# First block's inversion put ahead of the second block's preparation, its transfers on ScalarE's queue, and the last two steps' output sums taken one by one

## Chip, cores and metric

The kernel runs on one NeuronCore of a Trainium2 chip. The metric is the device time of one execution in microseconds (us). Five engines take part: PE (TensorE), DVE (VectorE), ACT (ScalarE), POOL (GpSimd) and SP (SyncE, which here only issues DMAs). Each engine works through its own list of instructions in the order of the program, and waits at the head of that list when an operand isn't there.

## What is computed

Three stages follow each other: a recurrence over 768 tokens for 4 x 8 heads of size 40, a router with eight experts, and a dense feed-forward layer.

```python
for t in range(S):                                   # recurrence, per head: state is 40 x 40
    y[:, :, t] = einsum('bhd,bhde->bhe', rt, state)
    Sa = einsum('bhde,bhe->bhd', state, at)
    state = state * wt[:, :, None, :] - einsum('bhd,bhe->bhde', Sa, bt) + einsum('bhd,bhe->bhde', vt, kt)
...
x = y.transpose(0, 2, 1, 3).reshape(B * S, H * D)    # 3072 x 320
expert = argmax(x @ w_gate); gate = softmax(x @ w_gate)[expert]
x = gate * (relu(x @ w1[expert]) @ w2[expert])       # at most 768 tokens an expert
h = x @ w_in
out = maximum(0.01 * h, h) @ w_out
```

## The kernel before

**The recurrence** (`attention`) is done in chunks of 32 tokens, so that most of it becomes small matmuls. A *block* i (0 to 5) is a set of four chunks g for both halves hf of the batch, which makes eight *steps* a block, s = 8i + 2g + hf, and 48 in all. A block goes through these stages:

- `load(n, h)` (n = 2i + hf, h the half of the chunks): SP issues the DMAs of w, KB and AE.
- `prep(n, h)`: on DVE two scans over w (L371, L375), a small copy WC (L372), a reciprocal (L373), a product Q (L374); then products on AE (L378, DVE or POOL) and on KB (L381, POOL or DVE).
- `gram(n, g)`: 16 small matmuls (L408), copies into mab (ACT), a DMA mab to Md in HBM, and masks on AE (L423 on DVE, L432 on POOL).
- `inverse_first` (block 0) or `inverse` (the others): Mu is loaded from Md; POOL makes Tt from it (L437); then the triangular inverse of 128 matrices of 32 x 32. For block 0 that is 56 DVE instructions in a row (L445, L447), each needing the one before. The result goes to Td by DMA; of block 0 a part also goes over Ta to Tad.
- `tbl(i, gp)` loads TB from Td. For block 0, `rtl` loads Rt from Tad with four DMAs, and `fix(hf, gp)` (L496, L498, L505) completes TB. Up to here a block's steps can't go on.
- The steps: `rv` (loads), `kbt`, `chain` (L562, copy X, L573 with TB, copies into MV, L590, L594: the state that step s + 2 needs), `output` (L610, L623, masks L631 on DVE or L637 on POOL) and `sums`.

`sums(s)` is called after each odd step and makes the outputs of the steps s and s + 1, that is both halves of the batch, in one run of 32 matmuls into `py` (three banks; half 0 uses banks 0 and 1, half 1 banks 1 and 2). After the last chunk of a block it multiplies py by Wt (L667), and `Router.add` does the routing of those rows: transposes, logits, position in the expert, and for each half two scatters by POOL (L904) into `xs` in HBM. The experts' stage begins by reading `xs` (L1036), when all scatters have landed.

**The order** on each engine comes from a list scheduler (`Sched`). Every `op` has a planned duration, keys that it reads and writes, a due time (`Q.due`, set by `when`), and a time before which it may not be planned (`Q.since`); `Sched.run` places the ops one by one on planned clocks, and `emit` writes them out in that order. So a planned clock decides only the order in which instructions stand on an engine; on the chip each one starts when its engine and its operands allow. In the kernel before, all DMAs of the recurrence are on SP (`QI = 'S'`); `dma` would plan a DMA on ACT at 0.06 us.

The AE and KB tiles have four buffers (n % 4), so blocks i and i + 2 share them; Mu and Tt are single.

Of the kernel before, what the change touches and what calls it, by code (L numbers as in the profile page):

```python
# [26 lines left out]
class Sched:  # L27
# [15 lines left out]
    def op(self, on, dur, fn, r=(), w=(), ring=None, done=0., grp=None, xfer=0., banks=(), sel=False, act=None):  # L43

        i = len(self.ops)
        deps = set()
        for k in r:
            if k in self.w:
                deps.add(self.w[k])
        for k in w:  # L50
            if k in self.w:
                deps.add(self.w[k])
            deps.update(self.r.get(k, ()))
        deps.discard(i)
        for k in r:
            self.r.setdefault(k, set()).add(i)
        for k in w:
            self.w[k] = i
            self.r[k] = set()
        on = on if isinstance(on, dict) else {on: dur}  # L60
        self.ops.append(dict(on=on, fn=fn, deps=deps, ring=ring, done=done, grp=grp, users=0, ps=None, xfer=xfer, banks=list(banks), due=self.due, since=self.since, slack=self.slack, sel=sel, act=act))
        return i
# [172 lines left out]
NV, QI, GS = 1, 'S', 0  # L235
SLACK0, LD0, LDS, PR0, PRS, LATEW, RV0, ZR0, ZRS, GR = 0.244, 0.0, 3.0, 18.956, 0.418, 0, 40.584, 52.618, 7.65, 1
NMV, NRE, NNI, NZ, NWT = 6, 6, 2, 4, 5
VROW = (5, 10)
EI = 'V'


# [34 lines left out]
def attention(ctx, tc, I, R, eng):  # L276
# [4 lines left out]
    Q = Sched(eng)  # L281
    op = Q.op
    V, A, P, T, S = eng
# [6 lines left out]
    def tiles(n, shape, name):  # L290
        return [cp.tile(shape, F32, name=f"{name}{i}") for i in range(n)]

    def copy(E, o, i):
        (E.copy if E is A else E.tensor_copy)(o, i)  # L294
# [4 lines left out]
    def alu(cols, on='VP'):  # L299
        return {e: t for e, t in (('V', .07 + .00104 * cols), ('P', .1 + .00219 * cols)) if e in on}  # L300
# [17 lines left out]
    Mu, Tt = tiles(1, [128, 32, 32], "Mu")[0], tiles(1, [128, 32, 32], "Tt")[0]  # L318
    tmps = tiles(3, [128, 256], "tmp")
    Ta = cp.tile([128, 16, 16], F32, name="Ta")  # L320
    R4 = cp.tile([128, 4, 8, 16], F32, name="Rt")
# [6 lines left out]
    py = ps.tile([128, 3, 512], F32, name="py")  # L328
    Mds = [dr.tile([8, 16, 32, 32], F32, name=f"Md{i}") for i in range(2)]
    Tds = [dr.tile([32, 4, 32, 32], F32, name=f"Td{i}") for i in range(2)]  # L330
    Tad = dr.tile([32, 4, 16, 16], F32, name="Tad")
# [8 lines left out]
        P.memset(maskZ, 0.0)  # L340
        P.iota(maskZ.bitcast(I32)[:, D:D + 1], [[0, 1]], base=NT, channel_multiplier=0)
    def dma(o, i, nb, r, w, on='S'):
        op(on, .48 if on == 'S' else .06, lambda E: E.dma_start(o, i), r, w, xfer=max(.18, nb / 360e3))

    def hold(i, fn):
        pass
# [87 lines left out]
    def inverse_first(i):  # L434

        dma(Mu, Mds[i % 2].rearrange("c u t s -> (c u) t s"), 1 << 19, [('Md', i % 2, c) for c in range(8)], ['Mu'])
        op('P', 1.47, lambda E: (E.affine_select(Tt, Mu, [[-1, 32], [1, 32]], ALU.is_gt, 0.0, base=0, channel_multiplier=0),  # L437
                                 E.memset(Tt.rearrange("u a b -> u (a b)")[:, 0:1024:33], -1.0)), ['Mu'], [('Tt', x) for x in range(3)])
        for x in range(2):
            for k in range(1, 15):  # L440
                m, o, c = 15 - k, 16 * x, 16 * x + k
                tv = tmps[x][:, 0:k * m].rearrange("u (a b) -> u a b", b=m)
                d = alu(k * m, EI)
                tt = Tt[:, o:o + k, c + 1:o + 16]
                op(d, 0, lambda E, tv=tv, k=k, o=o, c=c, m=m: E.tensor_tensor(tv, Mu[:, c:c + 1, c + 1:o + 16].broadcast_to([128, k, m]), Tt[:, o:o + k, c:c + 1].broadcast_to([128, k, m]), ALU.mult),  # L445
                   ['Mu', ('Tt', x)], [('tmp', x)])
                op(d, 0, lambda E, tv=tv, tt=tt: E.tensor_tensor(tt, tt, tv, ALU.subtract), [('tmp', x)], [('Tt', x)])  # L447
        op(ev(256), 0, lambda E: copy(E, Ta, Tt[:, 0:16, 0:16].rearrange("u a b -> u b a")), [('Tt', 0)], ['Ta'])
        dma(Tds[i % 2].rearrange("u q s t -> (u q) s t"), Tt, 1 << 19, [('Tt', x) for x in range(3)], [('Td', i % 2)], QI)
        dma(Tad.rearrange("u q s t -> (u q) s t"), Ta, 1 << 17, ['Ta'], ['Tad'], QI)  # L450

    def when(s):
        Q.due = START + STEP * s
# [1 line left out]
    def inverse(i):  # L455
        dma(Mu, Mds[i % 2].rearrange("c u t s -> (c u) t s"), 1 << 19, [('Md', i % 2, c) for c in range(8)], ['Mu'])
        cuts = [(VROW[0], VROW[1], 'V'), (0, VROW[0], 'V'), (VROW[1], 31, 'P')] if VROW[0] else [(0, VROW[1], 'V'), (0, 0, 'V'), (VROW[1], 31, 'P')]
        tk = [('Tt', x) for x in range(3)]
# [18 lines left out]

    def rtl():
        for q in range(4):
            dma(R4[32 * q:32 * q + 16].rearrange("s m u t -> s (m u) t"), Tad[:, q].rearrange("u s t -> s u t"), 80000, ['Tad'], [('Rt', m, q) for m in range(4)], QI)  # L480

    def tbl(i, gp):
        dma(TB4[:, gp].rearrange("s h u t -> s (h u) t"), Tds[i % 2][16 * gp:16 * gp + 16].rearrange("u q s t -> (q s) u t"), 262144,
            [('Td', i % 2)], [('TB', 2 * gp + h) for h in range(2)], QI if not i else 'S')

    def fix(hf, gp):
        m = 2 * gp + hf
# [148 lines left out]
            if pm:  # L636
                op('P', .62, lambda E, o=o, j=j: E.tensor_tensor(RE[o:o + 64, j], RE[o:o + 64, j], maskP[o:o + 64].unsqueeze(1).broadcast_to([64, 8, 32]), ALU.mult), ['mask'], [('REs', s % NRE, j, par) for par in range(2)])  # L637

    def sums(s):

        i, g, _, _ = info(s)
        def fy(E):
            for p in range(8):
                for j in range(2):
                    for hf in range(2):
                        b, col = place(hf, 2 * p + j)
                        q = 32 * ((g + 2 * hf) % 4)
                        x, z = REs[(s + hf) % NRE], Zs[(s + hf) % NZ]
                        E.matmul(py[q:q + 32, b, col:col + 40], x[:, j, p, :], z[:, p, ZC[j]:ZC[j] + 40], start=True, stop=True)  # L649
        keys = []  # L650
        for u in (s, s + 1):
            keys += [('Zo', u % NZ, h, j) for h in range(2) for j in range(2)] + [('Zs', u % NZ, j) for j in range(2)]
            keys += [('REo', u % NRE, j) for j in range(2)] + [('REs', u % NRE, j, par) for j in range(2) for par in range(2)]
        op('T', 1.45, fy, keys, [('py', hf, g) for hf in range(2)], banks=[('py', b) for b in range(3)], act=4000)
        if g == 3:
            for hf in range(2):
                n = 2 * i + hf
                xk = []
                for bb in range(2):
                    x = (2 * n + bb) % R.NXB  # L660
                    xk.append(x)
                    u = 8 * bb
                    while u < 8 * bb + 8:
                        b, col = place(hf, u)
                        m = min(8 * bb + 8 - u, 12 - col // 40)
                        op('V', .07 + .0416 * m, lambda E, x=x, u=u, b=b, col=col, m=m, bb=bb, n=n:
                           E.tensor_tensor(R.xbs[x][:, 40 * (u - 8 * bb):40 * (u - 8 * bb) + 40 * m], py[:, b, col:col + 40 * m], Wts[n % NWT][:, u:u + m, :].rearrange("p h e -> p (h e)"), ALU.mult),  # L667
                           [('py', hf, k) for k in range(4)] + [('Wt', n % NWT, h, j) for h in range(2) for j in range(2)], [('xb', x, u)], banks=[('py', b)])
                        u += m
                R.add(Q, psum, copy, ev, hf, i, xk)  # L670
# [40 lines left out]
    for m, t in enumerate(NIs):  # L711
        for j in range(2):
            r = RHO[j]
# [4 lines left out]
    for i in range(6):  # L718
        if i < 5:
            for h in range(2):  # L720
                for n in (2 * i + 2, 2 * i + 3):
                    when(8 * i + DPREP[2 * h + n % 2])
                    load(n, h)
                    prep(n, h)
                    for g in (2 * h, 2 * h + 1):
                        gram(n, g)
            inverse(i + 1)
            when(8 * i + DTURN)
            turn(2 * i + 2)
            turn(2 * i + 3)  # L730
        for c in range(8):
            s = 8 * i + c
            _, g, hf, n = info(s)
            when(s)
            if c % 4 == 0:
                tbl(i, g // 2)
                if s == 0:
                    rtl()
            if not i and g % 2 == 0:
                fix(hf, g // 2)  # L740
            Q.since = RV0 if 2 <= s < 8 else 0.
            rv(s)
            Q.since = 0.
            kbt(s)
            chain(s)
            if i == 0 and c < 4:
                Q.since = ZR0 + ZRS * c
                for e in (2 * c, 2 * c + 1):
                    R.zero_region(Q, e, maskZ, [('X', s % 2), ('xbt', 3), ('xbg', 3)] + [('xb', 3, u) for u in range(16)])
                Q.since = 0.  # L750
            when(s + DOUT)
            output(s)
            if s % 2:
                sums(s - 1)
    Q.run()
    Q.emit(lambda: T.matmul(py[:, 2, 320:448], R.one, R.one, start=True, stop=True))
# [704 lines left out]
```

## Time and profile before

| what | value |
|---|---|
| time, median of 3 runs | 1145.58 us (1144.32 to 1146.79) |
| the profiled execution | 1142.32 us, span of its instructions 1140.6 us |
| granted TensorE clock, mean | 0.928 |
| busy, of the span | PE 84%, DVE 69%, ACT 53%, POOL 43% |
| recurrence | from 0 to some 530 us |
| experts and dense layer | from 544 us (read of xs) to the end |

PE's share is high because of the second part, where it hardly pauses. In the recurrence the work of all engines is made of short instructions with waits between them, and there one reads, stretch by stretch, which engine had nothing to do and what ended its wait.

### The profile page before, as it was taken

To read this page: it belongs to the slowest core of one execution; us is meant where nothing else is said; L and a number is where in the kernel's file an instruction comes from. 1 tells how busy PE (TensorE), PEld (TensorE's weight loads), DVE (VectorE), ACT (ScalarE), POOL (GpSimd) and SP (SyncE) were. 2 spreads that over 40 slices of the span, in tenths; PEclk is the share of its full clock that TensorE was granted. 3 is DMA by queue.
4 is the path that set the end of the run, shared out by engine and by line. 5 is a ranking of instruction groups with operands and counts; after the bars stand their busy time and mean duration, and the time that the engine had idled before them with its cause. 6 is when DMAs were issued, how large, how long until landed. Compare 5 with 4: busy or idle time off the path is not lost.

```text
span 1140.6 us, 32337 instructions
## 1 busy us (share of the span) xinstructions
PE 959.8 (84%) x13219; PEld 848.1 (74%) x13219; DVE 791.2 (69%) x1856; ACT 605.2 (53%) x1428; POOL 487.0 (43%) x578
## 2 busy tenths in 40 slices
PE   4565677867777767887789999999999999999997
PEld 3454566656565656675678888989989999999997
DVE  8995878999989968643577777886754444444453
ACT  6135478758768668886434434434433333333343
POOL 7334434646636537121066555561949191010100
PEclk9767789879979889999789999999999999999999
DMA  7539575455445432430666666664211010000000
GB/s 211 195 77 238 137 184 135 134 133 162 133 104 151 131 73 75 107 106 20 205 186 184 200 196 197 198 173 124 81 35 47 24 24 24 1 20 5 24 13 15
DMA packets 134059, 127.82 MB, mean 112 GB/s; under 512 B 90768, under 2 KB 98576, under 8 KB 133904
## 3 DMA queue, kind: packets, MB, share of 16 engines
q1 hardware_dynamic: 131600, 117.79, 36.7%
q0 software_dynamic: 2304, 7.89, 1.9%
q8 instruction: 106, 1.74, 0.6%
q14 instruction: 49, 0.40, 0.1%
HBM read 101.48 MB, written 24.20 MB: 110 GB/s over the span
## 4 chain that ended last, share of the span: by engine, by line
PE 28%; issue 7%; DVE 6%; DMA 4%; POOL 3%; ACT 2%; SPq 1%; DVEq 0%; POOLq 0%; ACTq 0%
PE ph L1015 14%; PE oy L1222 3%; PE oy L1221 3%; PE oy L1220 3%; DMA wc<-cvm 2%; DVE wq L981 1%; PE y L1080 1%; PE y L1083 1%; POOL cvm L1118 1%; POOL cvm L1117 1%; POOL cvm L1119 1%; PE otr L1222 1%; PE otr L1220 1%; PE otr L1221 1%; DMA wa<-cvm 1%
## 5 line engine op out<-in xcount | busy, mean ns | idle before, releaser
L1015 PE MATMUL ph<-xt,wq 128*128 128x512 f32 (+2 forms) x1408 | 311.7, 365 | 4.0 <-DVE xt L1056 3.8
L1015 PEld LDWEIGHTS ph<-xt,wq 128*128 128x128 f32 x1408 | 248.8, 190 | 33.9 <-DVE xt L1056 4.7
L1200 DVE TENSOR_TENSOR gf<-gf,ph 128x512 f32<-128x512 f32 (+1 forms) x112 | 68.3, 610 | 98.9 <-ACT gf L1199 98.5
L1204 DVE TENSOR_TENSOR gl<-gf,gh 128x512 fp32r<-128x512 f32 (+1 forms) x112 | 76.7, 685 | 70.1 <-ACT gh L1203 70.1
L1199 ACT ACTIVATE gf<-ph 128x512 f32<-128x512 f32 (+1 forms) x112 | 60.0, 535 | 109.3 <-PE ph L1015 108.9
L1230 POOL DMA_INDIRECT out_dram<-ob,gid x24 | 23.9, 995 | 218.5 <-ACT ob L1229 213.3
L294 ACT COPY Z<-tr 40x512 f32<-40x512 f32 x192 | 100.4, 539 | 31.1 <-PE tr L610 29.1
L1203 ACT CAST gh<-gf 128x512 fp32r<-128x512 f32 (+1 forms) x112 | 62.7, 559 | 96.6 <-DVE gf L1200 96.6
L1066 ACT ACTIVATE gh<-ph 128x448 fp32r<-128x448 f32 x64 | 34.9, 545 | 121.4 <-PE ph L1015 121.4
L1222 PE MATMUL oy<-wo,gl 128*128 128x320 f32 x288 | 89.2, 310 | 0.2 <-DVE gl L1204 0.2
L1221 PE MATMUL oy<-wo,gh 128*128 128x320 f32 x288 | 88.9, 309 | 0.0
L1220 PE MATMUL oy<-wo,gh 128*128 128x320 f32 x288 | 88.8, 308 | 0.0
L1080 PE MATMUL y<-gh,wo 128*128 128x448 f32 x192 | 73.8, 384 | 6.2 <-DVE Y L1087 6.2
L610 PE MATMUL tr<-ident,MV 128*104 128x128 f32 x384 | 63.8, 297 | 17.8 <-ACT NI L294 6.8
L473 DVE TENSOR_TENSOR Tt<-Tt,tmp 128x30 f32<-128x30 f32 (+22 forms) x275 | 71.8, 290 | 0.7
L432 POOL TENSOR_TENSOR AE<-AE,maskP 32x256 f32<-32x256 f32 x40 | 30.2, 758 | 97.8 <-ACT AE L294 88.3
L1083 PE MATMUL y<-gl,wo 128*128 128x448 f32 x192 | 71.5, 372 | 0.0
L408 PE MATMUL tr<-AE,KB 128*64 128x64 f32 x704 | 37.3, 277 | 35.5 <-DVE AE L378 20.8
L649 PE MATMUL py<-Z,RE 128*32 128x40 f32 x1536 | 47.7, 226 | 22.4 <-DVE RE L631 16.9
L471 DVE TENSOR_TENSOR tmp<-Mu,Tt 128x30 f32<-128x30 f32 (+22 forms) x275 | 64.7, 265 | 0.5
L637 POOL TENSOR_TENSOR RE<-RE,maskP 64x256 f32<-64x256 f32 x24 | 18.6, 776 | 105.7 <-ACT RE L294 103.1
L631 DVE TENSOR_TENSOR RE<-tr,maskP 64x128 f32<-64x128 f32 x144 | 41.4, 288 | 31.7 <-PE tr L623 26.2
(182 smaller groups left out, 2372.1 us busy)
## 6 DMA issues: line engine op xcount, KB each, us to landing
KB<-in_kbT_dram SPq DMA_DIRECT2D x24, 512.0 KB, 6.2
RE<-in_rT_dram SPq DMA_DIRECT2D x48, 256.0 KB, 3.7
AE<-in_aT_dram SPq DMA_DIRECT2D x20, 512.0 KB, 9.2
raw<-in_wo_dram SPq DMA_DIRECT2D x16, 640.0 KB, 4.9
raw<-in_wqa_dram SPq DMA_DIRECT2D x16, 512.0 KB, 5.3
w<-in_wT_dram SPq DMA_DIRECT2D x24, 264.0 KB, 3.0
xs<-xb SPq DMA_DIRECT2D x8, 563.5 KB, 9.9
win<-xs SPq DMA_DIRECT2D x8, 563.5 KB, 8.3
```

What stands on the lines that cost most here:

```text
L294: (E.copy if E is A else E.tensor_copy)(o, i)
L471: op(e, d, lambda E, tv=tv, k=k, lo=lo, h=h, m=m: E.tensor_tensor(tv, Mu[:, k:k + 1, k + 1:].broadcast_to([128, h - lo, m]), Tt[:, lo:h, k ...
L473: op(e, d, lambda E, tv=tv, k=k, lo=lo, h=h: E.tensor_tensor(Tt[:, lo:h, k + 1:], Tt[:, lo:h, k + 1:], tv, ALU.subtract), [('tmp', x)], [t ...
L610: E.transpose(c['t'][0:104, q, :], MV[:, 4 * h + q], ident)
L1015: T.matmul(ph, l, r, start=k == 0, stop=k == 7)
L1080: T.matmul(y[c], hi, gh, start=m == 0, stop=False)
L1083: T.matmul(y[c], hi, gl, start=False, stop=m == 7)
L1200: V.tensor_tensor(gf, gf, ph, ALU.max)
L1204: V.tensor_tensor(gl, gf, gh.bitcast(F32), ALU.subtract)
L1220: T.matmul(o, gh[:, sl], w[:, 0:320], start=m == 0, stop=False)
L1221: T.matmul(o, gh[:, sl], w[:, 320:640], start=False, stop=False)
L1222: T.matmul(o, gl[:, sl], w[:, 0:320], start=False, stop=m == 15)
```

## The change

Three things are changed. `Q.since` is set to `PR1 = 38.6` around the preparation of the second block (i = 1, n = 2 and 3), so that none of its `prep` operations is planned before 38.6 on the planned clock; its loads are not held. The DMAs that follow the first block's inversion (Td, Tad, the first TB, the four Rt) are issued by ACT in place of SP, and a DMA issued by ACT is now planned at 0.48 us as on SP. In `sums` the halves are a parameter: for the steps 46 and 47 it is called after each step's output with one half, 16 matmuls, and its own banks.

```diff
+PR1 = 38.6
...
-        op(on, .48 if on == 'S' else .06, lambda E: E.dma_start(o, i), r, w, xfer=max(.18, nb / 360e3))
+        op(on, .48, lambda E: E.dma_start(o, i), r, w, xfer=max(.18, nb / 360e3))
...
-        dma(Tds[i % 2]..., Tt, 1 << 19, [('Tt', x) for x in range(3)], [('Td', i % 2)], QI)
-        dma(Tad..., Ta, 1 << 17, ['Ta'], ['Tad'], QI)
+        dma(Tds[i % 2]..., Tt, 1 << 19, [('Tt', x) for x in range(3)], [('Td', i % 2)], 'A')
+        dma(Tad..., Ta, 1 << 17, ['Ta'], ['Tad'], 'A')
...  (rtl: QI becomes 'A')
-            [('Td', i % 2)], [('TB', 2 * gp + h) for h in range(2)], QI if not i else 'S')
+            [('Td', i % 2)], [('TB', 2 * gp + h) for h in range(2)], 'A' if not i and not gp else 'S')
...
-    def sums(s):
+    def sums(s, hfs=(0, 1)):
...
-                    for hf in range(2):
+                    for hf in hfs:
...
-        op('T', 1.45, fy, keys, [('py', hf, g) for hf in range(2)], banks=[('py', b) for b in range(3)], act=4000)
+        op('T', 1.45 if len(hfs) > 1 else 1.15, fy, keys, [('py', hf, g) for hf in hfs], banks=[('py', b) for b in (range(3) if len(hfs) > 1 else ((0, 1), (1, 2))[hfs[0]])], act=2000 * len(hfs))
...
                     load(n, h)
+                    Q.since = 0. if i else PR1
                     prep(n, h)
+                    Q.since = 0.
...
-            if s % 2:
+            if s >= 46:
+                sums(46, (hf,))
+            elif s % 2:
                 sums(s - 1)
```

## Rows read from the trace of the kernel before

**Rows 1.** The page: busy tenths of DVE in 40 equal slices of the span.
```profile
DVE  8995878999989968643577777886754444444453
```

**Rows 2.** Windows: stretch, its length, each engine's busy us (instructions); clock, DMA, GB/s.
```profile
39.00:54.50 15.50, 8.19 (x170) 7.97 (x169) 15.03 (x13) 0.61 (x3) 8.10 (x5) 0.92 0.88 318
54.50:65.30 10.80, 3.95 (x55) 3.69 (x55) 10.71 (x59) 3.13 (x9) 3.64 (x3) 0.64 0.05 11
65.30:85.50 20.20, 14.35 (x227) 12.90 (x227) 19.49 (x30) 7.47 (x26) 6.82 (x6) 0.66 0.51 105
85.50:98.10 12.60, 5.18 (x306) 4.59 (x297) 0.00 (x0) 5.43 (x19) 1.40 (x2) 0.67 0.78 197
```

**Rows 3.** Timeline (start us, duration, engine, line; brackets: idle before, releaser): first steps.
```profile
84.86 0.73 PE L496 MATMUL tr<-Rt,TB 16*32 16x16 f32 x64
...
91.97 1.31 PE L573 MATMUL ch<-X,TB 32*32 32x40 f32 x64
...
98.14 0.99 DVE L594 TENSOR_TENSOR MV<-ch,WC 40x320 f32<-40x320 f32 x2 [12.68 <-PE ch L590]
```

**Rows 4.** Timeline of DVE and POOL around the first block's inversion.
```profile
37.79 1.18 DVE L423 TENSOR_TENSOR AE<-ch,maskP 32x128 f32<-32x128 f32 x4
42.35 1.37 POOL L437 TENSOR_SCALAR_AFFINE_SELECT Tt<-Mu 128x1024 f32<-128x1024 f32 x1 [10.65 <-DMA Mu<-Md]
54.51 0.23 DVE L445 TENSOR_TENSOR tmp<-Mu,Tt 128x14 f32<-128x14 f32 x2
58.40 0.69 DVE L378 TENSOR_TENSOR AE<-AE,Q 64x512 f32<-64x512 f32 x1
62.24 2.94 DVE L447 TENSOR_TENSOR Tt<-Tt,tmp 128x14 f32<-128x14 f32 x2
73.41 3.17 DVE L378 TENSOR_TENSOR AE<-AE,Q 64x512 f32<-64x512 f32 x1
73.86 2.17 POOL L381 TENSOR_TENSOR KB<-KB,w 128x1024 f32<-128x1024 f32 x1
```

**Rows 5.** DMA issues between 36 and 100 us: KB each, median us from issue to landing.
```profile
Td<-Tt SPq DMA_DIRECT2D x1, 512.0 KB, 2.7
TB<-Td SPq DMA_DIRECT2D x2, 256.0 KB, 3.5
...
Rt<-Tad SPq DMA_DIRECT2D x4, 32.0 KB, 2.8
```

**Rows 6.** Timeline of SP's queue: DMA issues, from the first block's inversion on.
```profile
65.20 0.33 SPq L343 DMA_DIRECT2D Td<-Tt  x1
...
69.43 4.32 SPq L343 DMA_DIRECT2D Md<-mab  x2
...
74.33 0.47 SPq L343 DMA_DIRECT2D TB<-Td  x1
74.84 3.09 SPq L343 DMA_DIRECT2D Rt<-Tad  x4
...
93.30 1.63 SPq L343 DMA_DIRECT2D Mu<-Md  x1
...
427.15 0.34 SPq L343 DMA_DIRECT2D Mu<-Md  x1
```

**Rows 7.** Timeline of ACT: its first work after the first steps' X copies.
```profile
60.35 0.52 ACT L294 COPY AE<-tr 32x128 f32<-32x128 f32 x2 [20.55 <-PE tr L408]
```

**Rows 8.** Timeline of the recurrence's end: last masks, sums, scatters, read of xs.
```profile
527.38 1.23 DVE L631 TENSOR_TENSOR RE<-tr,maskP 64x128 f32<-64x128 f32 x4 [1.02 <-PE tr L623]
527.50 0.72 POOL L637 TENSOR_TENSOR RE<-RE,maskP 64x256 f32<-64x256 f32 x1 [9.79 <-ACT RE L294]
528.32 1.47 PE L649 MATMUL py<-Z,RE 128*32 128x40 f32 x64
...
536.85 1.08 POOL L904 DMA_INDIRECT xs<-xb,rii  x1 [8.63 <-DVE rm L880]
...
544.36 0.34 SPq L1036 DMA_DIRECT2D win<-xs  x1
```

More of the change, by code (lines that the diff above doesn't have):

```diff
@@ L448, in inverse_first @@
         op(ev(256), 0, lambda E: copy(E, Ta, Tt[:, 0:16, 0:16].rearrange("u a b -> u b a")), [('Tt', 0)], ['Ta'])
-        dma(Tds[i % 2].rearrange("u q s t -> (u q) s t"), Tt, 1 << 19, [('Tt', x) for x in range(3)], [('Td', i % 2)], QI)
-        dma(Tad.rearrange("u q s t -> (u q) s t"), Ta, 1 << 17, ['Ta'], ['Tad'], QI)
+        dma(Tds[i % 2].rearrange("u q s t -> (u q) s t"), Tt, 1 << 19, [('Tt', x) for x in range(3)], [('Td', i % 2)], 'A')
+        dma(Tad.rearrange("u q s t -> (u q) s t"), Ta, 1 << 17, ['Ta'], ['Tad'], 'A')
     def when(s):
@@ L479, in rtl @@
         for q in range(4):
-            dma(R4[32 * q:32 * q + 16].rearrange("s m u t -> s (m u) t"), Tad[:, q].rearrange("u s t -> s u t"), 80000, ['Tad'], [('Rt', m, q) for m in range(4)], QI)
+            dma(R4[32 * q:32 * q + 16].rearrange("s m u t -> s (m u) t"), Tad[:, q].rearrange("u s t -> s u t"), 80000, ['Tad'], [('Rt', m, q) for m in range(4)], 'A')
     def tbl(i, gp):
         dma(TB4[:, gp].rearrange("s h u t -> s (h u) t"), Tds[i % 2][16 * gp:16 * gp + 16].rearrange("u q s t -> (q s) u t"), 262144,
-            [('Td', i % 2)], [('TB', 2 * gp + h) for h in range(2)], QI if not i else 'S')
+            [('Td', i % 2)], [('TB', 2 * gp + h) for h in range(2)], 'A' if not i and not gp else 'S')
     def fix(hf, gp):
@@ L650, in sums @@
         keys = []
-        for u in (s, s + 1):
+        for u in [s + hf for hf in hfs]:
             keys += [('Zo', u % NZ, h, j) for h in range(2) for j in range(2)] + [('Zs', u % NZ, j) for j in range(2)]
             keys += [('REo', u % NRE, j) for j in range(2)] + [('REs', u % NRE, j, par) for j in range(2) for par in range(2)]
-        op('T', 1.45, fy, keys, [('py', hf, g) for hf in range(2)], banks=[('py', b) for b in range(3)], act=4000)
+        op('T', 1.45 if len(hfs) > 1 else 1.15, fy, keys, [('py', hf, g) for hf in hfs], banks=[('py', b) for b in (range(3) if len(hfs) > 1 else ((0, 1), (1, 2))[hfs[0]])], act=2000 * len(hfs))
         if g == 3:
-            for hf in range(2):
+            for hf in hfs:
                 n = 2 * i + hf
```

## The prediction, made before the change was run

> **What bounds the kernel now.** I read the page first, then the windows of the stretch that the change touches, then the timelines of DVE, POOL, SP, PE and ACT in it, and last the end of the recurrence. On the page one looks at DVE: close to full in the first slices and again and again up to the eighteenth, at four to six tenths in the last ten [rows 1]. So the recurrence leans on DVE, the later stages on PE. The change touches only the recurrence; the later stages start when its last scatters have landed, and I let them shift as a whole with it, by one for one.
>
> In the windows one sees what the front looks like. DVE works 15.03 of 15.5 us, 10.71 of 10.8 and 19.49 of 20.2, and then for 12.6 us not at all [rows 2]. The hole from 85.5 to 98.1 is ended by step 0's state update L594, which waited 12.68 us for PE's L590 [rows 3]. Behind that stands this chain: the inversion ran from 54.51 to 65.18, although POOL had finished its Tt at about 43.9 [rows 4]; Td was issued at 65.20 and landed 2.7 us later [rows 5], but the load of TB stood behind other transfers in SP's queue (two Md issues alone took 4.32 us, wait included) and left only at 74.33, the four Rt at 74.84 to 77.93 [rows 6]; PE took up fix at 84.86 and the first steps' L573 at 91.97 [rows 3]. The second block's way is the other limit: its preparation kept DVE busy to 85.5, and its Mu left at 93.30 [rows 2, 6]. From there the blocks follow each other at (427.15 - 93.30)/4 = 83.5 us a block [rows 6]. A block's steps free the buffers for the block after the next, and its inverse must be done before its own steps; so I take a shift of the front to be handed on to the end, whatever the period.
>
> **The edits, one by one.**
>
> *Inversion first.* DVE is free at 37.79 + 1.18 = 38.97; Tt is ready at 42.35 + 1.37 plus a short memset, 43.9 [rows 4]. With the preparation held back DVE waits 5.0 us there for nothing: that is the price. The inversion takes 62.24 + 0.34 - 54.51 less the 0.69 of one product of the preparation that lies in it, 7.4 us (its last pair, 2.94 in the trace, is counted at 0.34, about what the pairs before it took) [rows 4]. So it ends near 51.3 and Td can leave 13.9 us earlier than 65.20. The preparation costs 15.03 + 10.71 + 19.49 = 45.2 us of DVE time in the trace, less 10.0 for the inversion with its held last pair, 35.2; it then ends at 51.3 + 35.2 = 86.5 without the steps, or 89.1 if the 2.6 us that the inversion lost come up elsewhere: 1 to 4 us later than the 85.5 of now.
>
> *Transfers on ACT.* Seven issues move: Td 0.33, Tad, TB 0.47, four Rt 3.09, some 4.3 us at SP's durations [rows 6]. The trace shows no DMA issued by ACT. From below I take nothing, from above those 4.3 us plus a wait of 2.7 us for Td to land at the head of ACT's list. ACT's cover is its idle time of 20.55 us before 60.35 [rows 7]; the chain falls into 51 to 61, so most is hidden. If the cover is gone, what stands behind are the copies of the second block's first grams, and behind these its Md transfers: up to 7 us on the way to Mu. I take zero, as ACT's idle row is the nearest. For the first block I get: Td landed at 51.3 + 0.3 + 2.7 = 54.3, TB at 58.3, Rt, issued one after another from about 55, at 61 [rows 5, 6]. PE's order is the other term: half of the second block's grams may stand ahead of fix, and these come with half of the 35.2 us, at 69. So fix comes at 61 to 69 in place of 84.86, and L573, 7.1 us behind it as now [rows 3], at 68 to 76 in place of 91.97. SP is rid of the same 4.3 us; as its next Md waits for copies and not for SP's time, I give that nothing, and at the most 2 us on Mu.
>
> The Trainium skill ("DMA: Bandwidth & Descriptors", section "Issuing engines are not separate DMA queues") says that transfers of all issuing engines run on the same 16 DMA engines, and that another issuer only saves the time of issuing. By it the move would be worth no more than issue time; the row beside it shows Td landed 6.4 us before TB was issued, which is order in a queue and not bandwidth. The sum below is the same either way.
>
> *What it is worth.* Step 0's chain no longer decides when DVE goes on. The 12.6 us hole is the gain that is there, since steps 0 to 3 then give DVE work during the second block's Mu transfers; the 5.0 us wait at 39 is paid: 12.6 - 5.0 = **7.6 us**. Bounds: more than the hole, if the holding of DVE by POOL goes as well. One product takes 0.69 at 58.40 and 3.17 at 73.41, where POOL's KB product of 2.17 runs beside it [rows 4]; there are four such KB products, so at most 4 x 2.17 = 8.7 us, 16.3 in all. On the other side nothing of the hole is filled and the 5.0 us are paid, with up to 3 us from ACT: 8 us slower. Both unknowns are bounded from both sides; I take the hole alone, since it is read directly.
>
> The Trainium skill ("SBUF — State Buffer", section "SBUF: two separate sides") speaks against the larger value: DVE and POOL share a pair of ports by an exclusive lock, held for a whole instruction. The trace agrees where a product takes 3.17 us beside POOL's 2.17. By that rule the lost time goes with POOL's products wherever they are put, and the gain stays at 7.6.
>
> *Sums taken one by one.* At the end, step 46's mask on POOL ends at 527.50 + 0.72 = 528.22 and step 47's on DVE at 527.38 + 1.23 = 528.61; the 64 matmuls of both take 1.47 [rows 8]. With half 0 alone its 32 are done at 528.22 + 0.74 = 528.96 in place of 529.79: **0.8 us** earlier. The four scatters stand one behind the other on POOL from 536.85 and the last one's landing lets xs be read at 544.36 [rows 8], so the first one's start carries. Bounds: zero, if DVE must wait for bank 1, which PE then fills for half 1; 2 us, if step 46's copies are also put ahead of step 47's. The matmuls stay as many; two more waits cost nothing visible.
>
> *Sum.* 7.6 + 0.8 = 8.4. Against the profiled execution: 1142.3 - 8.4 = 1133.9. That execution is 3.3 us below the median of the runs, so the median comes to **1137** us.
>
> **The rivals.**
>
> *Second block late* (slower). The inversion of block 0 is early, but the second block's Mu is what step 8 waits for. Its preparation ends 1 to 4 us later by itself, and DVE work of steps 0 to 3 comes in between, as do ACT's waits (up to 7). It decides as soon as Mu leaves later than 93.30 by more than the inverse of block 1 gains from having fewer steps beside it. For it: DVE is full before 85.5. Against it: those steps' work is taken out of the time behind Mu. Price: 5.0 of new wait plus 3 on ACT, less 0.8 at the end: about +7, 1153; chance 0.21.
>
> *A wash.* Both limits move by nearly the same, or the new order loses later what it wins at the front: within 3 us, 1143 to 1148; chance 0.15. It includes that the change doesn't do what it says: 38.6 is on the planned clock, and if Mu is planned later than that, the scans still stand ahead of the inversion; then only the 6.4 us of SP's queue remain, on a chain that PE's grams hide.
>
> *Everything recovered.* The hole, and most of the 8.7 us: 16 us, 1129; chance 0.13.
>
> The forecast, 4 to 12 us faster (1133 to 1142), has 0.51.
>
> **How the numbers follow.** 0.2% is 2.3 us, about what a measurement of this kernel can tell from no change. Faster: 0.51 + 0.13 = 0.64. Within: 0.15. Slower: 0.21. The forecast's own range is 1133 to 1142. The range reaches down into the full recovery (1127) and up to where half of the slower case lies (1150), which leaves out some 0.05 below and 0.12 above.
>
> **What would show it.** Right: L445 starts near 44 and Td leaves near 51 to 52 from ACT; fix near 61 to 69; no hole of over 5 us in DVE between 51 and the second block's inverse; Mu of block 1 within some 4 us of 93.3; the last block's Mu about 7 us before 427.15; xs read near 536. Wrong: scans of the preparation ahead of L445; ACT waiting at a DMA while copies of grams stand behind it; block 1's Mu after 100; or an earlier front that the later blocks give back, seen as a Mu of the last block at 427 or later.

## The result, and the profile after

| | before | after |
|---|---|---|
| time, median (lowest to highest), same chip | 1144.95 us (1137.55 to 1149.22, 10 runs) | 1131.84 us (1127.32 to 1137.91, 10 runs) |
| ratio, 95% interval | | 0.9904 [0.9882, 0.9927] |
| the profiled execution, its span | 1142.32, 1140.6 us | 1136.73, 1135.0 us |
| Mu of block 1 / block 2 / block 5 leaves | 93.30 / 185.56 / 427.15 | 90.02 / 177.01 / 419.66 |
| xs read | 544.36 | 539.70 |

By the ratio the changed kernel is faster by 11.0 us of the 1144.95 (8.4 to 13.5 by the interval; the two medians lie 13.1 apart); the forecast was 8.4. The profiled execution of after is 4.9 us above the median of its runs and that of before 2.6 below, so late marks of the two traces compare only to some us. The early ones repeat better: in three kernels with the same order up to the last steps (inv_only, inv_again and no_act, below) Mu of block 1 leaves at 94.15, 93.76 and 93.37. I rest on the early ones. In after all line numbers are one higher up to L638 (L562 is L563), L667 is L668, L904 is L909, L1036 is L1041.

The windows of after in the four stretches of [rows 2] (stretch, length, busy us of PE, PEld, DVE, ACT, POOL; clock, DMA share, GB/s):

```profile
39.00:54.50 15.50, 12.78 (x249) 12.55 (x235) 11.34 (x62) 1.04 (x3) 3.47 (x3) 1.00 0.97 342
54.50:65.30 10.80, 2.72 (x46) 2.59 (x48) 10.52 (x11) 2.49 (x8) 4.05 (x4) 0.52 0.80 153
65.30:85.50 20.20, 13.13 (x303) 11.68 (x300) 17.23 (x31) 8.41 (x28) 8.84 (x7) 0.67 0.63 159
85.50:98.10 12.60, 8.78 (x312) 7.65 (x314) 7.01 (x11) 6.99 (x24) 0.87 (x2) 0.77 0.72 186
```

One sees DVE's hole half filled, 7.01 us where there were none, and the price in the first line, 11.34 us where there were 15.03. Over the four stretches DVE is busy for 46.10 us in place of 45.23: that alone is next to nothing. But it gets more done in that time, as the part on the prediction shows: its instructions lose less to those of POOL beside them. The DVE timeline says the rest (start, duration, instruction; in brackets the idle time before and who ended it):

```profile
43.12 0.26 DVE L446 TENSOR_TENSOR tmp<-Mu,Tt 128x14 f32<-128x14 f32 x2 [4.02 <-POOL Tt L438]
49.52 0.31 DVE L448 TENSOR_TENSOR Tt<-Tt,tmp 128x14 f32<-128x14 f32 x2
49.74 1.25 DVE L372 TENSOR_TENSOR_SCAN W<-w,d 128x528 f32<-128x528 f32 x1
52.61 2.56 DVE L375 TENSOR_TENSOR Q<-W,rC 128x512 f32<-128x512 f32 x1
...
84.80 1.26 DVE L372 TENSOR_TENSOR_SCAN W<-w,d 128x528 f32<-128x528 f32 x1
88.37 1.01 DVE L595 TENSOR_TENSOR MV<-ch,WC 40x320 f32<-40x320 f32 x2 [0.95 <-PE ch L591]
90.64 1.26 DVE L372 TENSOR_TENSOR_SCAN W<-w,d 128x528 f32<-128x528 f32 x1
...
99.25 0.29 DVE L472 TENSOR_TENSOR tmp<-Mu,Tt 128x30 f32<-128x30 f32 x2 [5.35 <-POOL Tt L460]
```

The inversion stands first (43.12 to 49.83), the preparation behind it, and with its grams' masks it ends at 84.8, no later than before. Step 0's update L595 comes at 88.37, 9.8 us ahead of [rows 3]. What fills the hole is mostly the third block's scans, two from 84.80 and two from 90.64. Only the second pair is work done earlier: the second block has four pairs of scans, and before had a fifth one, the third block's first, ahead of the hole.

```profile
81.08 1.26 DVE L371 TENSOR_TENSOR_SCAN W<-w,d 128x528 f32<-128x528 f32 x1
...
82.98 1.26 DVE L375 TENSOR_TENSOR_SCAN w<-w,d 128x528 f32<-128x528 f32 x1
```

A new gap of 5.35 us stands before the second block's inverse, which waits for POOL's Tt.

The transfers, ACT's queue:

```profile
49.88 0.35 ACTq L344 DMA_DIRECT2D Td<-Tt  x1
...
56.73 0.43 ACTq L344 DMA_DIRECT2D TB<-Td  x1
60.38 0.34 ACTq L344 DMA_DIRECT2D Rt<-Tad  x1
61.25 0.31 ACTq L344 DMA_DIRECT2D Rt<-Tad  x1
67.98 0.31 ACTq L344 DMA_DIRECT2D Rt<-Tad  x1
71.04 0.31 ACTq L344 DMA_DIRECT2D Rt<-Tad  x1
```

and PE, where fix (L497) and step 0's L574 stand:

```profile
77.66 1.98 PE L409 MATMUL tr<-AE,KB 128*64 128x64 f32 x32 [2.50 <-DVE AE L379]
79.57 1.05 PE L497 MATMUL tr<-Rt,TB 16*32 16x16 f32 x64
...
84.45 0.75 PE L574 MATMUL ch<-X,TB 32*32 32x40 f32 x32 [0.31 <-ACT TB L295]
```

Td left 15.3 us earlier than in [rows 6], but TB could be issued only 6.85 us later, the last two Rt 11 and 14 us after TB; fix came 5.3 us earlier than in [rows 3], not 16 to 24. The last Rt landed 2.8 us after its issue, near 73.9; from there to 79.57 fix stood on PE behind two grams that waited for their AE.

### The profile page after: what moved, and what is told of

Same layout as the page of the kernel before. It is cut to its first block, busy times and chain, and to the rows that moved or that the text cites. A ratio compares the mean times of both kernels' runs of the same rounds, so it can differ in the third digit from the quotient of the medians.

```text
span 1135.0 us, 32381 instructions
## 1 busy us (share of the span) xinstructions
PE 958.4 (84%) x13241; PEld 846.5 (75%) x13241; DVE 785.5 (69%) x1855; ACT 605.6 (53%) x1430; POOL 489.3 (43%) x577
## 4 chain that ended last, share of the span: by engine, by line
PE 20%; issue 14%; DVE 6%; POOL 5%; DMA 4%; ACT 2%; SPq 1%; POOLq 0%; DVEq 0%; ACTq 0%
PE ph L1020 10%; PE oy L1227 2%; PE oy L1226 2%; PE oy L1225 2%; DMA wc<-cvm 2%; POOL cvm L1123 1%; DMA wa<-cvm 1%; POOL cvm L1124 1%; POOL cvm L1122 1%; DVE wo L994 1%; DVE gf L1205 1%; PE y L1085 1%; DVE wq L986 1%; PE otr L1227 1%; PE otr L1226 1%
## 5 line engine op out<-in xcount | busy, mean ns | idle before, releaser
L474 DVE TENSOR_TENSOR Tt<-Tt,tmp 128x30 f32<-128x30 f32 (+24 forms) x275 | 72.5, 292 | 0.7
L472 DVE TENSOR_TENSOR tmp<-Mu,Tt 128x30 f32<-128x30 f32 (+23 forms) x275 | 67.9, 277 | 5.8 <-POOL Tt L460 5.4
L638 POOL TENSOR_TENSOR RE<-RE,maskP 64x256 f32<-64x256 f32 x24 | 19.3, 806 | 102.7 <-ACT RE L295 102.6
L611 PEld LDWEIGHTS tr<-ident,MV 128*104 128x104 f32 x384 | 44.6, 141 | 24.1 <-ACT NI L295 8.3
L295 ACT COPY MV<-ch 32x160 f32<-32x160 f32 x192 | 54.4, 284 | 15.2 <-PE ch L574 12.3
```

The costliest lines, as they stand in the source:

```text
L472: op(e, d, lambda E, tv=tv, k=k, lo=lo, h=h, m=m: E.tensor_tensor(tv, Mu[:, k:k + 1, k + 1:].broadcast_to([128, h - lo, m]), Tt[:, lo:h, k ...
L474: op(e, d, lambda E, tv=tv, k=k, lo=lo, h=h: E.tensor_tensor(Tt[:, lo:h, k + 1:], Tt[:, lo:h, k + 1:], tv, ALU.subtract), [('tmp', x)], [t ...
L611: E.transpose(c['t'][0:104, q, :], MV[:, 4 * h + q], ident)
```

## Experiments

Kernels with one letter ran on one chip, beside the kernel before; kernels of different chips are compared by their ratios.

| chip | kernel | median, us | before there | ratio, 95% interval |
|---|---|---|---|---|
| A | inv_only | 1123.82 | 1138.90 | 0.9872 [0.9836, 0.9907] |
| A | act_only | 1138.97 | 1138.90 | 1.0004 [0.9977, 1.0030] |
| A | split_only | 1135.44 | 1138.90 | 0.9975 [0.9949, 1.0001] |
| A | no_split | 1126.94 | 1138.90 | 0.9895 [0.9860, 0.9930] |
| B | no_act | 1128.27 | 1137.66 | 0.9916 [0.9890, 0.9943] |
| B | rt_sp | 1125.26 | 1137.66 | 0.9885 [0.9848, 0.9922] |
| B | dve_prep | 1140.29 | 1137.66 | 1.0025 [1.0003, 1.0048] |
| B | pe_step | 1134.98 | 1137.66 | 0.9982 [0.9960, 1.0003] |
| C | inv_again | 1129.99 | 1142.51 | 0.9889 [0.9850, 0.9928] |
| C | fill_inv | 1131.10 | 1142.51 | 0.9900 [0.9862, 0.9938] |
| C | mu_pool | 1131.39 | 1142.51 | 0.9898 [0.9858, 0.9937] |
| C | fill_mu | 1133.68 | 1142.51 | 0.9926 [0.9901, 0.9950] |

### Each part alone: inv_only, act_only, split_only, and the whole without the last part

```diff
 inv_only: before, and
+PR1 = 38.6
+                    Q.since = 0. if i else PR1
                     prep(n, h)
+                    Q.since = 0.
 act_only: before, and the seven DMAs 'A' in place of QI, .48 for any issuer
 split_only: before, and sums(s, hfs), called with one half for s >= 46
 no_split: after, and sums(s - 1) for all odd s, as before
```

> The kernel before with the second block's preparation held to 38.6 and nothing else: all DMAs on SP, the last sums paired. Theory (what pays is DVE's order: the inversion ahead of the preparation, so that DVE's 12.6 us hole is filled): the larger part of the gain is here, 5 to 9 us faster than before, ratio 0.992 to 0.996; block 1's Mu leaves 3 us earlier or more, the last block's Mu 6 to 9 us before 427.15. Rival (SP's queue is what holds the first steps, ACT's is what frees them): 0 to 2 us faster, ratio above 0.998, since Td, TB and Rt again stand behind Md transfers.

> The kernel before with only the first block's seven transfers issued by ACT; the preparation stands ahead of the inversion, the last sums are paired. Theory (DVE's order pays): within 2 us of before, ratio 0.998 to 1.002, because the inversion still ends near 65 and the second block's Mu still leaves near 93. Rival (queues pay): 4 to 8 us faster, with fix some 6 us ahead of 84.86.

> The kernel before with only the last two steps' sums taken one by one; every engine's order up to the last two steps is that of before. Theory: the first scatter starts 0.8 us earlier (0 to 2), ratio 0.998 to 1.000; the last block's Mu at 427 as before. Rival (it moves more, since the order of the last copies changes too): 2 to 4 us faster.

> The changed kernel with its last sums paired again (inversion first, transfers on ACT). Theory: some 1 us slower than the changed kernel, so 0.991 to 0.995 of before. Rival (the sums carry a good part of the gain): 0.995 to 0.998.

The inversion put first gives all of the gain by itself: by the ratio 14.6 us on chip A and 12.7 on chip C (inv_again). no_act, further down, has the same order up to the last steps and came to 0.9916, so ratios 0.004 apart can belong to one order. ScalarE's transfers alone give nothing (1.0004). Their trace shows why: on DVE the inversion still stands behind the scans (Td leaves at 65.31), and the hole stays.

```profile
85.50:98.10 12.60, 7.00 (x349) 6.18 (x346) 0.00 (x0) 3.94 (x14) 1.43 (x2) 0.70 0.84 185
```

In the same trace ACT shows the cost that the prediction bounded and then took as zero: between two copies that wait for grams, TB leaves at 78.50, later than SP's 74.33 in [rows 6], with all Rt behind it.

```profile
78.49 0.26 ACT L294 COPY AE<-tr 32x128 f32<-32x128 f32 x1 [4.29 <-PE tr L408]
78.50 0.38 ACTq L343 DMA_DIRECT2D TB<-Td  x1
...
86.07 0.32 ACTq L343 DMA_DIRECT2D Rt<-Tad  x1
```

In inv_only, where SP issues everything, the four Rt leave at once and PE takes up fix 8 us earlier than in after. SP, then PE:

```profile
50.55 0.33 SPq L344 DMA_DIRECT2D Td<-Tt  x1
...
56.40 0.39 SPq L344 DMA_DIRECT2D TB<-Td  x1
56.84 3.64 SPq L344 DMA_DIRECT2D Rt<-Tad  x4
...
94.15 1.17 SPq L344 DMA_DIRECT2D Mu<-Md  x1
```

```profile
71.53 1.05 PE L497 MATMUL tr<-Rt,TB 16*32 16x16 f32 x64 [0.17 <-issue]
```

Yet Mu of block 1 left no earlier than before (94.15), and the second block's inverse began on DVE at 102.09, as before (102.19). The gain stood in the next mark: Mu of block 2 at 178.54 in place of 185.56 (179.78 and 175.67 in inv_again and no_act). no_split beside it is 3.1 us slower than inv_only (its runs 1124.48 to 1129.17, those of inv_only 1121.87 to 1125.96), so ScalarE's transfers bring nothing in either company, and may cost a little.

The last part is seen best between the last step's L573 and the first scatter, which it alone touches. In before the last L573 stands at 517.52, the first scatter at 536.85 [rows 8], 19.33 us behind it. The two in split_only:

```profile
514.92 0.49 PE L573 MATMUL ch<-X,TB 32*32 32x40 f32 x32 [1.06 <-ACT MV L294]
```

```profile
533.15 1.08 POOL L906 DMA_INDIRECT xs<-xb,rii  x1 [9.53 <-DVE rm L882]
```

That is 18.23 us, **1.1 us** less. After (514.12 to 532.36) shows 18.24, no_split and inv_again, which keep the pairs, 19.34 and 19.33. The way there isn't the one that was forecast. PE in split_only, first the run of half 0, then that of half 1:

```profile
523.68 1.33 PE L649 MATMUL py<-Z,RE 128*32 128x40 f32 x32 [0.73 <-POOL RE L637]
...
527.89 1.23 PE L649 MATMUL py<-Z,RE 128*32 128x40 f32 x29
```

Half 0's run ends 10.1 us behind the last L573 in place of the 12.3 of both, 2.2 earlier, because ACT also takes step 46's last copies (RE at 522.25) ahead of step 47's. But its logits (L871) begin only at 528.92, behind half 1's run, and 1.1 us are left at the scatter. The whole-time ratio of 0.9975 is compatible with it and too wide to say more.

### Without ScalarE, and with the Rt alone back on SP: no_act, rt_sp

```diff
 no_act: after, QI in place of 'A' in all seven DMAs, dma's planned durations as before
 rt_sp: after, and only in rtl
-            dma(R4[...], Tad[...], 80000, ['Tad'], [('Rt', m, q) for m in range(4)], 'A')
+            dma(R4[...], Tad[...], 80000, ['Tad'], [('Rt', m, q) for m in range(4)], QI)
```

> The change with the transfers of the first block left on SP: inversion first, and the last two steps' sums one by one. Inversion first alone came to 0.9872 of before, the last sums alone to 0.9975, ScalarE's transfers alone to 1.0004 and, beside inversion first, to a loss of about 3 us. Theory (DVE's order carries the gain, ScalarE's transfers cost 2 to 4 us, the two remaining parts add): ratio 0.983 to 0.987, some 1120 to 1124 us where before takes 1139; fix near 71 to 72 us, Td issued by SP near 50. Rival (the order of DVE and the tail overlap, or ScalarE's loss was chance): 0.989 to 0.991 as the whole change.

> The change with only the four Rt loads back on SP; Td, Tad and the first TB stay on ScalarE. In the change the Rt stood on ScalarE between copies that waited for PE's grams and left at 60.4, 61.3, 68.0 and 71.0 us, and fix came at 79.6. Theory (it is the order on ScalarE that costs): Rt leave together at 57 to 61, fix near 71 to 74, and the time falls by 2 to 4 us against the whole change, ratio 0.984 to 0.988. Rival (Td on ScalarE, or the load of the DMA engines, holds fix): fix stays within 2 us of 79.6 and the ratio at 0.989 to 0.992.

With the Rt on SP and Td, Tad, TB still on ACT, the four Rt leave in one run of 3.54 us from 57.40, and fix comes at 70.40:

```profile
70.40 1.05 PE L497 MATMUL tr<-Rt,TB 16*32 16x16 f32 x64 [0.18 <-issue]
```

The first theory holds on the mark, 9.2 us earlier, but two things did it. The edit made the scheduler plan anew, and on PE fix now stands behind four of the second block's grams, in after behind six. In after the last Rt landed near 73.9: some 3.5 of the 9.2 us are the late Rt on ScalarE, some 5.7 are PE's order, planned with them. On the time it isn't shown: 0.9885 lies in the interval of after, and no_act, with fix at 71.48, came to 0.9916, outside what either theory of mine gave (0.983 to 0.987, or at most 0.991), though its interval reaches into the second. So fix 8 to 9 us earlier isn't worth anything that these runs can tell. The steps that follow find other waits: of the 9.2 us in rt_sp 5.5 are left at step 0's L574 (78.92 and 84.45), 4.6 at its update (83.81 and 88.37) and 0.4 where POOL starts the second block's Tt (97.51 and 97.95).

### Is the front's time handed on? dve_prep, pe_step

```diff
 dve_prep: after, ahead of the second block's first scan on VectorE
+            for _ in range(28 if n == 2 and h == 0 else 0):
+                E.memset(idle, 0.0)
 pe_step: after, ahead of step 0's L574 on PE
+            for _ in range(120 if s == 0 else 0):
+                E.matmul(py[:, 2, 320:448], R.one, R.one, start=True, stop=True)
```

> The change with 28 memsets of 128x256 of a spare tile on VectorE, about 7 us, put between the first block's inversion and the second block's preparation; nothing else differs. Theory of the prediction (VectorE's order at the front sets the second block's Mu, and a shift of the front is handed on to the end one for one): Mu of block 1 near 97 in place of 90, all later Mu about 7 us later, 5 to 7 us slower than the change, ratio 0.995 to 0.997. Rival (VectorE has slack there after the change, and the shift goes up in the hole that is filled before step 0's update): 0 to 2 us, ratio 0.990 to 0.992.

> The change with 120 matmuls of 128x128 into an unused part of a bank on PE just ahead of step 0's L574, some 7 us on the way of the first steps alone, behind the second block's grams; nothing else differs. Theory of the prediction (second block's Mu is the other limit, steps have some slack): Mu(1) stays at 90, its steps come 7 us later, and the time moves by 0 to 2 us, ratio 0.990 to 0.992. Rival (the first steps, by freeing the buffers for the block after the next and by their own place in the chain, carry the gain, as the lone inversion suggested, where Mu(1) was no earlier than before): 4 to 7 us slower, ratio 0.994 to 0.997.

The memsets took more than was planned, 10.85 us, and Mu of block 1 was issued 11.1 us later than in after. DVE, then SP:

```profile
50.61 10.85 DVE L375 MEMSET idle<- 128x256 f32 x28
```

```profile
101.13 1.42 SPq L345 DMA_DIRECT2D Mu<-Md  x1
```

The time went from a ratio of 0.9904 to 1.0025, which is 13.8 us (3.6 either way, from the two intervals). The 10.85 us lie within: time added at the front of DVE comes out at the end, about one for one. Every engine's order is that of after, so nothing else was changed. The slack of the rival isn't there.

In pe_step the 120 matmuls took 7.45 us, and the time rose by 0.0078 of the ratio, 8.9 us (3.5 either way). But this kernel doesn't separate what I meant it to separate: Mu(1) was to stay at 90 and went to 95.81. ACT shows how:

```profile
85.36 0.36 ACT L295 COPY mab<-tr 32x256 f32<-32x256 f32 x1 [0.47 <-DVE AE L424]
92.52 1.19 ACT L295 COPY MV<-ch 32x160 f32<-32x160 f32 x4 [6.79 <-PE ch L576]
93.62 0.36 ACT L295 COPY mab<-tr 32x256 f32<-32x256 f32 x1
```

The last copy of the second block's grams stands on ACT behind step 0's MV copies, and those wait for step 0's matmul. In after the same order stands at 84.86, 85.27 and 86.38. So the second block's Mu and the first steps are not two limits side by side, as the prediction has it: a late step 0 makes Mu late through ACT's order (step 0's L574, MV, the last mab, Md, Mu). pe_step shows that for a delay. In after the order costs the last mab 1.1 us at most (85.27 to 86.38), and an early step 0 brings Mu nothing: in inv_only L574 stands at 80.04 and the copies of mab are done at 85.6, but Mu stands on SP behind a load of MV from 89.71 on.

### Taking the waits away: inv_again, fill_inv, mu_pool, fill_mu

```diff
 inv_again: inv_only once more
 fill_inv: inv_only, and the first five operations of n == 2, h == 0 may be planned at once
+        hold = Q.since
+        Q.since = 0. if n == 2 and not h else hold
         op('V', .62, ... scan W ...)        (WC, 1/WC, Q, scan w follow)
+        Q.since = hold
 mu_pool: inv_only, and in inverse(i)
-        dma(Mu, Mds[i % 2]..., ['Mu'])
+        dma(Mu, Mds[i % 2]..., ['Mu'], 'P' if i == 1 else 'S')
 fill_mu: both
```

> The inversion put first and nothing else, once more, as the base of the three kernels beside it on the same chip. Both theories: ratio to before within 0.984 to 0.991, as in its first run (0.9872); Mu of block 1 issued at 94, behind a load of MV at which SP stands for some 4 us.

> Inversion first, and in VectorE's wait for Tt (4 us, from 39) the first five operations of the second block's preparation: two scans, WC, reciprocal, Q, 3.7 us by the rows of after (1.25, 0.17, 1.26, 0.25 and 0.8). Theory (the wait at 39 is paid with useful time, 5.0 us in the sum of the prediction, and every us of VectorE's work at the front is handed on): the preparation ends 3 to 4 us earlier and the time falls by 2 to 4 us against the inversion first alone, ratio lower by 0.002 to 0.0035. Rival (the front isn't VectorE's alone any more: SP's and ScalarE's order decides when Mu of block 1 leaves): Mu(1) stays at 94 and the time within 1 us. If the five take over 4.5 us, the inversion starts later, and what is won is that much smaller.

> Inversion first, and the Mu load of block 1 issued by GpSimd in place of SP; every other order is the same. In the lone inversion Mu(1) left at 94.15, though the last copies into mab were done at 85.6: on SP it stood behind a load of MV that waited for its buffer (89.71, 4.33 us). Theory (that queue is the limit of the second block): Mu(1) leaves at 87 to 90, Tt is made 4 to 6 us earlier, and the time falls by 2 to 5 us against the inversion first alone. Rival (VectorE is busy with the third block's scans and the steps until then, its total work to the end decides): Mu(1) earlier, but the time within 1.5 us.

> Both edits together on the inversion first: the five operations of the preparation in VectorE's wait at 39, and Mu of block 1 issued by GpSimd. If the front's VectorE time and the queue ahead of Mu(1) are two separate waits: 5 to 8 us less than the inversion first alone, ratio to before 0.980 to 0.983. If one covers the other: no more than the better of the two alone, 0.983 to 0.986. If neither is on the way: 0.987.

The edits did in the trace what they were meant to do. fill_inv's five operations stand in DVE's wait, and the wait for Tt shrinks from 4.42 us (inv_again) to 1.16:

```profile
39.00 1.26 DVE L374 TENSOR_TENSOR_SCAN W<-w,d 128x528 f32<-128x528 f32 x1
...
41.91 0.69 DVE L377 TENSOR_TENSOR Q<-W,rC 128x512 f32<-128x512 f32 x1
43.76 0.26 DVE L449 TENSOR_TENSOR tmp<-Mu,Tt 128x14 f32<-128x14 f32 x2 [1.16 <-POOL Tt L441]
...
49.95 2.27 DVE L449 TENSOR_TENSOR tmp<-Mu,Tt 128x14 f32<-128x14 f32 x2
```

Part of it is lost at once: the scan's early end lets POOL's KB product start at 49.95 (2.23 us), inside the inversion, and the pair beside it takes 2.27 us where it takes 0.30 in inv_again. Still Mu(1) leaves at 89.72 in place of 93.76. But POOL starts Tt at 97.57 in place of 99.39, and the second block's inverse begins on DVE at 101.21 in place of 102.13: of the 4.0 us 0.9 are left. The median is 1131.10 against 1129.99: no gain, where 2 to 4 us were expected. mu_pool fails for another reason, and shows it. POOL issues Mu at 90.20, 3.6 us ahead of inv_again's SP, and Tt is made at 98.80 in place of 99.39. The DMA issues of mu_pool between 86 and 103 us (KB, median us to landing), then those of inv_again:

```profile
Mu<-Md POOLq DMA_DIRECT2D x1, 512.0 KB, 8.5
```

```profile
Mu<-Md SPq DMA_DIRECT2D x1, 512.0 KB, 5.5
```

Of the 3.6 us that Mu left earlier it lost 3.0 on the way. The DMA engines are busy for 0.93, 1.09 and 1.01 of the three stretches of 2 us from 90 to 96 in mu_pool (a transfer counts whole where it starts, so the share can pass 1); block 2's AE and the zeros of xs travel beside it. It isn't POOL's queue alone: in no_split SP issued the same Mu at 89.97, and it landed after 7.8 us. The Trainium skill ("DMA: Bandwidth & Descriptors", section "Issuing engines are not separate DMA queues") says that all issuers share the same 16 DMA engines; the traces agree, with 8.5 us from POOL and 7.8 from SP. And fill_mu, both edits together, is at 0.9926, no better than either alone: its Mu landed at 94.2, but Tt starts at 97.44, since POOL's list has an AE product ahead of it that waits for its own load.

So a us added at the front costs one, and a us of wait removed was not seen to give one. Up to the second block's inverse the traces show where it goes: most of Mu's head start is lost in the DMA engines. Why nothing is left of the rest stays open; fill_inv, unlike mu_pool, also made the scheduler plan anew, so its orders differ in more than the five operations. For fill_inv the trace has the later marks ahead of inv_again by 4 to 7 us up to block 5's Mu (415.79 and 422.40), and by 3.5 at the read of xs; but inv_only and inv_again are the same kernel, and their traces differ there by 3.8 and 7.4 us (418.62 and 422.40; 533.99 and 541.39). A single trace doesn't carry the difference, and the medians say no gain.

None of these versions beats after for certain. The inversion first and nothing else, at 0.9872 and 0.9889, is at least as fast as the whole change at 0.9904, with the smallest edit.

## Why the prediction was right, point by point

- **The total** (8.4 us) was right in size, a little small: 11.0 measured, 8.4 to 13.5. Most of its marks held: L446 at 43.12 (said: near 44), Td at 49.88 (51 to 52; the inversion took 6.7 us, not 7.4), Mu(1) 3.3 us ahead of 93.30, the last Mu 7.5 us earlier (said: about 7). The mark at the read of xs did not: 539.70, not 536, in an execution that was itself above its median.
- **That ScalarE's part and SP's relief are worth nothing by themselves, and DVE's order carries the gain**, was right: 1.0004 against 0.9872. The wash rival (38.6 too late on the planned clock) didn't come up, since the first scan starts only at 49.74.
- **"The 12.6 us hole is the gain that is there"**: mis-sized, and the filling wrongly named. 7.01 us of it are filled, chiefly by the third block's scans and one step's update, not by steps 0 to 3; 4.02 us are paid at 39 (said: 5.0), and 5.35 us come back as a wait for the second block's Tt, so the mark "no hole of over 5 us" failed by a little. Up to 98.1 DVE is busy only 0.9 us longer for all this.
- **The holding of DVE by POOL, taken at nothing**, is the larger term. I added up what DVE's instructions from 39 to 98 took above the shortest with the same line, tiles and shape in their trace, where that was over 0.3 us; each of these has an instruction of POOL beside it. It gives 13.5 us before (13.5 in split_only too), 8.0 in after (7.9 in no_split) and 9.5 in inv_only. The bound of 8.7 for it was too low. So by 98.1 DVE got 6.4 us more work done, 0.9 by being busy longer and 5.5 by losing less. The sum 12.6 − 5.0 came near that because its errors offset each other; that is luck. How 6.4 us there become 11.0 at the end isn't worked out.

A copy of 16 columns, held, in before and in after; its shortest takes 0.15 to 0.18 us:

```profile
50.23 3.19 DVE L372 COPY WC<-W 128x16 f32<-128x16 f32 x1
```

```profile
58.97 2.14 DVE L373 COPY WC<-W 128x16 f32<-128x16 f32 x1
```

- **POOL's lock.** The prediction put the exclusive lock of the Trainium skill ("SBUF — State Buffer", section "SBUF: two separate sides") against a larger gain: the lost time would go with POOL's products wherever they are put. The four KB products do still hold DVE, now at other instructions (the Q product at 52.61 took 2.56 us where 0.69 is its shortest; in fill_inv it was a pair of the inversion). What it overlooked is that the new order changes what POOL does: before, two AE products of the second block ran on POOL (48.99 and 69.40, 3.5 us together), and in after all eight are on DVE, at 0.7 us apiece when nothing holds them.
- **Transfers on ACT, "I take zero"**: a step that failed, though the sum was spared by it. The row taken for cover, 20.55 us of idle [rows 7], ended at 60.35, and the chain was to be done by 61. Two durations were too short. Td and TB: 6.85 us pass from Td's issue to TB's, not 3.0, as the DMA engines are at 0.97 and 0.80 in after's first two windows, where before's Td left behind a stretch at 0.05 [rows 2]. The Rt: behind the cover stood the copies that the prediction names as the price, and two of four Rt left at 67.98 and 71.04. PE's order put six of the eight grams ahead of fix, not four. Fix at 79.57 in place of 61 to 69 follows from both; against rt_sp's 70.40 the Rt make some 3.5 us and PE's order some 5.7.
- **"The second block's way is the other limit"**: wrong as two limits. pe_step shows that a late step 0 delays Mu through ACT's order, and inv_only gains 14.6 us though its second block's inverse begins when it did before. In after Mu(1) leaves 3.3 us earlier, but POOL starts Tt at 97.95 in place of 99.45: half of it is lost in the transfer. The rule drawn from it, a shift of the front is handed on, held for added time (dve_prep) and wasn't seen for removed waits (fill_inv).
- **The rival on the other side**, the second block late, asked for a preparation that ends 1 to 4 us later. It ended at 84.8: the scans lost nothing to the held pair of the inversion, and DVE work of steps came in only behind it.
- **Sums one by one**: 0.8 said, 1.1 measured from the last L573 to the first scatter, in all kernels that have it. The size is right by luck: half 0's run came 2.2 us earlier (ACT's copies changed places, which the prediction has as its bound of 2 us), and the wait behind half 1's run took half of that back.

## What to carry to other kernels

A hole behind a full engine is often an order and not a dependence: look for the chain that stands behind other work although its operands are there, and put it first. Before a hole is taken as the gain, also add up what the busy instructions of that stretch take above their shortest, and ask which of them the new order will leave alone. A DMA issued by an engine that computes stands in that engine's list: count the copies ahead of it, and what they wait for, before its idle time is taken as cover. Where a scheduler plans the order, an edit to one transfer moves instructions on other engines too: compare the orders before a mark is put down to the edit. Before a wait is priced as a limit, see on the next engine in the chain whether the same work isn't ordered behind the thing that it is set against.

## What the runs showed of the hardware that was not expected

- The landing of one 512 KB transfer varies with the load: Td took 2.7 us in before, where it left behind a stretch at a DMA share of 0.05 [rows 2, 5], and 6.6 us in rt_sp, where the share from its issue to its landing is 0.91. Mu landed in 5.5 us in inv_again (issued at 93.76), in 7.8 in no_split (89.97, from SP) and in 8.5 in mu_pool (90.20, from POOL).
- 28 memsets of 128x256 on DVE, into one tile, took 10.85 us: 0.27 us each by the profile, and 0.12 us from one to the next.
- The same kernel's late marks differ by 4 to 7 us between two executions on two chips (Mu of block 5, the read of xs), its early ones by 0.4 us at the first inversion; medians of a kernel move by 7 us from chip to chip (before: 1137.66 to 1144.95), its ratio to before by 0.002.
- What follows the read of xs took 587.3 to 596.3 us in the fourteen traces, and not by kernel: inv_only and no_act have the same order ahead of it up to the last steps, and show 587.3 and 596.2. So whole times of single executions differ by several us that no edit at the front made.
